# Float64 weights split in 512-column pieces, with the steps of the split dealt out anew over three engines

## Chip, cores and metric

The kernel runs on one core of one Trainium2 chip. The metric is the device time of one execution, in microseconds (us). Before the change three runs took 2179.05, 2179.7 and 2180.8 us, median 2179.7 us.

## What is computed

The reference chains an attention and two feed-forward layers over 4 x 576 = 2304 tokens of 512 numbers:

```python
attn_out = _attn_ref(q, k, v)        # 8 heads of 64; window 32, heads 4-7 with stride 4
x = attn_out.transpose(0, 2, 1, 3).reshape(B * S, H * D)     # [2304, 512]
# _moe_ref
xn = x / sqrt(mean(x * x) + 1e-6) * rms_g
g = xn @ w_gate                      # w_gate, w_val [512, 1536]
x = (g * sigmoid(g) * (xn @ w_val)) @ w_out                  # w_out [1536, 512]
# _moe2_ref
P = exp(x @ wg); 8 times: normalise P over experts and over tokens
out = sum over 8 experts of P[:, e] * (relu(x @ w1[e]) @ w2[e])
```

The three matrices of the first feed-forward layer (w_gate, w_val, w_out) reach the kernel as float64 numbers, 8 bytes each. All others are float32.

## The kernel before

TensorE multiplies in a rounded 32-bit format (float32r). To keep float32 accuracy each operand is split into a high part and a low part, and each product takes three passes: high x high, high x low, low x high (`PASSES`). A float64 weight is first made into a float32 one on the chip, then split.

**The weights.** The three matrices are cut into 36 weights of 128 x 512 numbers, numbered 0 to 35. `moe1_weights` makes them in this order: for each third fg = 0, 1, 2 of the inner dimension, four of w_gate (g0 to g3), four of w_val (v0 to v3), and four of w_out. A name such as v02 is row block 0 of w_val, third 2; o8 is row block 8 of w_out. `split_double` (from L241) makes one of them. Numbers 0 to 25 are *wide*: one DMA of 512 KB (L250) brings all 512 columns into a tile of the pool wx. Numbers 26 to 35 (g22, g32, v02 to v32, o8 to o11) are *narrow*: two DMAs of 256 KB each (L262) bring half of the columns into a staging tile, three of which are in the pool stg and two in apool. In both cases the conversion then runs in two halves of 256 columns:

- ScalarE takes the absolute value of the float64's upper word (L271) into a scratch tile m;
- VectorE clamps it (L272), shifts and masks it (L274) and puts sign and top bit back (L277);
- ScalarE scales the lower word (L281) and GpSimd adds it to m (L282), which is now the float32 weight;
- the high part is a rounded copy of m: on ScalarE (L284) for even numbers, on GpSimd (L286) for odd ones;
- the low part is m minus the high part (L289): on GpSimd for every third number, on VectorE for the others.

The scratch m of weights 0 to 11 and of the narrow ones is one of three 256-column buffers of apool. Weights 12 to 25 use a wx tile as scratch, one for two weights (`m_slot`).

**The order of the work.** Every engine runs its instructions in the order of its own queue. A scheduler sets these orders when the program is built, with a simulated timeline; only SP, which issues the loads, is scheduled by hand-written code order from L501 to L586. The program order around the change: attention of block 0 and 1 (tiles 0 to 4; `att_tile`) among the first weights; the first third of both blocks (`gemm_h` makes the products pg and pv and the hidden h, `gemm_out` the output product po); the second third; the last third of block 0; attention of block 2 (tiles 5 to 7); the last third of block 1. After that come blocks 2 to 7, with all weights resident, and then the second layer, which loads and splits float32 weights (L458 to L489).

```python
def gemm_h(blk, f):      # 4 row blocks x 3 passes each for pg, then pv
    ...
        nc.scalar.activation(hf, pg[:, :n], AF.Silu)
        nc.vector.tensor_tensor(out=hf, in0=pv[:, :n], in1=hf, op=ALU.mult)
```

pg_1_11 is the gate product of block 1 for inner block 11, po_0_2_0 the first output product of block 0 in the last third.

Of the kernel before, what the change touches and what calls it, by code (L numbers as in the profile page):

```python
# [8 lines left out]
F32 = mybir.dt.float32  # L9
F32R = mybir.dt.float32r  # L10
AF = mybir.ActivationFunctionType
ALU = mybir.AluOpType
# [5 lines left out]
P = 128  # L18
# [8 lines left out]
LEAST, MOST = (struct.unpack("f", struct.pack("I", w))[0] for w in (0x38100000, 0x47EFFFFF))  # L27
# [5 lines left out]
def attention_moe_kernel(  # L33
# [14 lines left out]
    nc = tc.nc  # L48
# [6 lines left out]
    stg = ctx.enter_context(tc.tile_pool(name="stg", bufs=3))  # L55
# [14 lines left out]
    apool = ph1.enter_context(tc.tile_pool(name="apool", bufs=1))  # L70
# [167 lines left out]

    m_slot = []

    def split_double(pool, src, name, number, hi_eng, lo_eng):  # L241

        wide = number < 26
        w = pool.tile([P, 2, 512], F32R, tag="w", name=f"w_{name}")
        if wide:
            st = wx.tile([P, 2, 512], F32R, tag="w", name=f"sd_{name}")
            raw = st.rearrange("p s n -> p (s n)").bitcast(U32)
            nc.sync.dma_start(raw.bitcast(U64), src)  # L250
            if number >= 12:
                if number % 2 == 0:
                    m_slot.append(wx.tile([P, 2, 512], F32R, tag="w", name=f"m_{name}").bitcast(F32))
                scratch = m_slot[-1][:, number % 2, :].rearrange("p (j n) -> p j n", j=2)
        for j in range(2):
            cols = slice(256 * j, 256 * j + 256)
            if wide:
                words = raw[:, 512 * j : 512 * j + 512]
            else:
                pool_st, bufs = (stg, 3) if (2 * number + j) % 5 < 3 else (apool, 2)  # L260
                words = pool_st.tile([P, 512], U32, tag="st", name=f"sd_{name}_{j}", bufs=bufs)
                nc.sync.dma_start(words.bitcast(U64), src[:, cols])  # L262
            words = words.rearrange("p (n t) -> p n t", t=2)
            low, high = words[:, :, 0], words[:, :, 1]
            if wide and number >= 12:
                mf = scratch[:, j, :]
            else:
                mf = apool.tile([P, 256], F32, tag="m", name=f"m_{name}_{j}", bufs=3)
            m = mf.bitcast(U32)

            nc.scalar.activation(mf, high.bitcast(F32), AF.Abs)  # L271
            nc.vector.tensor_scalar(out=mf, in0=mf, scalar1=LEAST, scalar2=MOST, op0=ALU.max, op1=ALU.min)  # L272

            nc.vector.tensor_scalar(  # L274
                out=m, in0=m, scalar1=3, scalar2=0x3FFFFFF8, op0=ALU.logical_shift_left, op1=ALU.bitwise_and
            )
            nc.vector.scalar_tensor_tensor(  # L277
                out=m, in0=high, scalar=0xC0000000, in1=m, op0=ALU.bitwise_and, op1=ALU.bitwise_or
            )

            nc.scalar.activation(low, low, AF.Copy, scale=2.0**-29)  # L281
            nc.gpsimd.tensor_tensor(out=m, in0=m, in1=low, op=ALU.add)  # L282
            if hi_eng is nc.scalar:
                nc.scalar.copy(w[:, 0, cols], mf)  # L284
            else:
                hi_eng.tensor_scalar(  # L286
                    out=w[:, 0, cols], in0=mf, scalar1=1.0, scalar2=1.0, op0=ALU.mult, op1=ALU.mult
                )
            lo_eng.tensor_tensor(out=w[:, 1, cols], in0=mf, in1=w[:, 0, cols].bitcast(F32), op=ALU.subtract)  # L289
        return w  # L290

    def split_weight(pool, src, name, *how):
        if src.dtype == U64:
            return split_double(pool, src, name, *how)
        st = stg.tile([P, 512], F32, tag="st", name=f"st_{name}", bufs=3)
        nc.sync.dma_start(st, src)
        w = pool.tile([P, 2, 512], F32R, tag="w", name=f"w_{name}")
        nc.scalar.copy(w[:, 0, :], st)
        nc.vector.tensor_tensor(out=w[:, 1, :], in0=st, in1=w[:, 0, :].bitcast(F32), op=ALU.subtract)
        return w  # L300
# [3 lines left out]
    def moe1_weights():  # L304
        cnt = 0

        def one(dst, key, pool, src, name):
            nonlocal cnt
            dst[key] = split_weight(
                pool, src, name, cnt,  # L310
                (nc.scalar, nc.gpsimd)[cnt % 2], (nc.gpsimd, nc.vector, nc.vector)[cnt % 3],
            )
            cnt += 1

        for fg in range(3):
            for dst, src, nm in ((gw, w_gate, "g"), (vw, w_val, "v")):
                for kt in range(4):
                    one(
                        dst, (kt, fg), wr if fg == 0 else wx,
                        src[kt * P : kt * P + P, fg * 512 : fg * 512 + 512], f"{nm}{kt}{fg}",  # L320
                    )
                    yield
            for f in range(4 * fg, 4 * fg + 4):
                one(ow, f, wr if fg < 2 else wx, w_out[f * P : f * P + P, :], f"o{f}")
                yield
# [572 lines left out]
```

## Time and profile before

| | |
|---|---|
| median of three runs | 2179.7 us (2179.05 to 2180.8) |
| the profiled execution | 2179.37 us |
| its span (first to last instruction) | 2177.6 us |
| outside the span | 1.8 us |
| mean granted clock of TensorE | 0.98 |

Engines in the profile: PE is TensorE's matrix multiplication, PEld its weight loads (beside PE), DVE VectorE, ACT ScalarE, POOL GpSimd, SP SyncE, which issues DMAs. A busy time counts only instructions that compute. PEclk is the clock that TensorE was granted, as a share of its full 2.4 GHz. L272 is line 272 of the kernel. A wait is put down to what came last.

### The profile page before, as it was taken

The numbers are of one execution on the slowest core, as the hardware profiler recorded it, in microseconds if no ns is written. First come the engines' busy times: TensorE is split into PE (matmuls) and PEld (weight loads), VectorE is DVE, ScalarE is ACT, GpSimd is POOL, SyncE is SP. The second block draws the span as 40 slices with busy tenths as digits, with TensorE's granted clock in tenths as the row PEclk, the third lists the DMA queues.
The fourth block names the chain that finished last, engine by engine and source line by source line (L and its number), as shares of the span: only waits on it lengthen the run. The fifth ranks groups of instructions, "written<-read, shape, count | busy, mean of one in ns | idle before, by whom it ended". The sixth has DMA issues, their size and how long they took to land.

```text
span 2177.6 us, 32755 instructions
## 1 busy us (share of the span) xinstructions
PE 2095.7 (96%) x12546; PEld 1904.3 (87%) x12546; DVE 1240.5 (57%) x2159; ACT 901.4 (41%) x1952; POOL 772.4 (35%) x853
## 2 busy tenths in 40 slices
PE   4899999999998699999999999999999999999999
PEld 3788999999986589998998899899989998899887
DVE  7987333423463565665656466656656565566553
ACT  4655443434354233443334444433434444344431
POOL 3774111111275242433333334333332334333320
PEclk7899999999998899999999999999999999999999
DMA  9233212210133111221122122212221122122110
GB/s 267 94 110 110 59 56 58 68 45 26 56 117 113 49 63 49 78 78 54 63 88 87 50 68 78 73 55 67 78 85 66 63 78 68 53 75 78 59 40 34
DMA packets 83246, 160.92 MB, mean 74 GB/s; under 512 B 10384, under 2 KB 18192, under 8 KB 83088
## 3 DMA queue, kind: packets, MB, share of 16 engines
q1 hardware_dynamic: 76128, 140.63, 20.3%
q10 hardware_dynamic: 6960, 18.19, 3.0%
q8 instruction: 98, 1.61, 0.3%
q14 instruction: 60, 0.49, 0.1%
HBM read 149.34 MB, written 9.44 MB: 73 GB/s over the span
## 4 chain that ended last, share of the span: by engine, by line
PE 87%; DVE 5%; DMA 3%; issue 2%; ACT 1%; POOL 1%; SPq 1%; ACTq 0%; POOLq 0%; DVEq 0%
PE py L742 36%; PE pa L685 18%; PE pb L685 9%; PE po L342 6%; PE pg L368 6%; PE pv L368 5%; PE pc L685 5%; PE psX L182 1%; DMA sd_v<-in_w_val 1%; PE psS L138 1%; DMA st_w<-in_w 1%; DMA first<-in_kt 0%; DVE m_o L272 0%; DVE m_g L277 0%; DMA sd_g<-in_w_gate 0%
## 5 line engine op out<-in xcount | busy, mean ns | idle before, releaser
L742 PE MATMUL py<-w,h 128*128 128x512 f32 x3456 | 867.4, 395 | 1.2 <-DVE acc L763 0.6
L742 PEld LDWEIGHTS py<-w,h 128*128 128x128 f32 x3456 | 648.6, 189 | 120.9 <-DVE acc L763 1.0
L489 POOL TENSOR_TENSOR w<-st_w,w 128x512 fp32r<-128x512 f32 x184 | 238.1, 1314 | 351.9 <-ACT w L488 342.2
L763 DVE SCALAR_TENSOR_TENSOR acc<-py,Pm,acc 128x512 f32<-128x512 f32 x264 | 194.1, 748 | 273.0 <-PE py L742 272.6
L685 PE MATMUL pa<-x_b,w 128*128 128x384 f32 x1152 | 257.2, 340 | 12.4 <-ACT w L471 7.1
L458 POOL TENSOR_TENSOR w1s<-w1r 128x256 f32<-128x256 f32 x92 | 75.0, 816 | 511.6 <-DVE w L472 511.6
L685 PE MATMUL pa<-x_t,w 128*128 128x384 f32 x1152 | 244.6, 337 | 0.0
L685 PEld LDWEIGHTS pa<-x_b,w 128*128 128x128 f32 x1152 | 208.5, 190 | 25.5 <-ACT w L471 8.7
L685 PEld LDWEIGHTS pa<-x_t,w 128*128 128x128 f32 x1152 | 206.7, 188 | 14.2 <-ACT pq L714 0.2
L368 PE MATMUL pv<-xn,w_v 128*128 128x320 f32 (+1 forms) x1152 | 185.9, 300 | 6.3 <-DVE hf L381 2.2
L383 POOL TENSOR_TENSOR h<-hf,h 128x256 fp32r<-128x256 f32 (+1 forms) x96 | 80.4, 839 | 314.3 <-ACT h L382 311.6
L488 ACT CAST w<-st_w 128x512 fp32r<-128x512 f32 x184 | 108.6, 621 | 198.5 <-PE pa L685 85.5
L368 PE MATMUL pg<-xn,w_g 128*128 128x320 f32 (+1 forms) x1152 | 182.6, 299 | 4.6 <-ACT xn L232 4.3
L342 PE MATMUL po<-h,w_o 128*128 128x320 f32 (+1 forms) x1152 | 178.4, 299 | 6.0 <-DVE w_o L289 3.3
L368 PEld LDWEIGHTS pv<-xn,w_v 128*128 128x128 f32 x1152 | 163.4, 190 | 11.1 <-DVE hf L381 3.1
L342 PEld LDWEIGHTS po<-h,w_o 128*128 128x128 f32 x1152 | 160.5, 189 | 12.0 <-DVE w_o L289 3.7
L368 PEld LDWEIGHTS pg<-xn,w_g 128*128 128x128 f32 x1152 | 163.2, 191 | 7.5 <-issue 6.1
L472 DVE TENSOR_TENSOR w<-w1r,w 128x512 fp32r<-128x512 f32 x92 | 111.8, 1215 | 50.0 <-ACT w L471 49.8
L472 DVE TENSOR_TENSOR w<-w1s,w 128x512 fp32r<-128x512 f32 x184 | 123.4, 696 | 27.6 <-ACT w L471 25.9
L471 ACT CAST w<-w1s 128x512 fp32r<-128x512 f32 x184 | 111.3, 620 | 61.6 <-PE pc L685 18.2
L697 ACT ACTIVATE h<-pq 128x384 fp32r<-128x384 f32 x96 | 50.4, 525 | 184.2 <-DVE pq L726 183.5
L685 PE MATMUL pb<-x_t,w 128*128 128x384 f32 x576 | 126.5, 338 | 0.0
(157 smaller groups left out, 2734.1 us busy)
## 6 DMA issues: line engine op xcount, KB each, us to landing
st_w<-in_w SPq DMA_DIRECT2D x184, 256.0 KB, 2.7
w1r<-in_w SPq DMA_DIRECT2D x184, 256.0 KB, 2.8
vbd<-in_vt ACTq DMA_DIRECT2D x30, 256.0 KB, 3.8
kbd<-in_kt ACTq DMA_DIRECT2D x30, 208.0 KB, 3.8
sd_g<-in_w_gate SPq DMA_DIRECT2D x10, 512.0 KB, 7.0
xr<-x2d SPq DMA_DIRECT2D x12, 384.0 KB, 3.5
sx<-x2d SPq DMA_DIRECT2D x24, 192.0 KB, 2.4
out<-acc SPq DMA_DIRECT2D x18, 256.0 KB, 2.1
```

Source lines behind the costliest of these rows:

```text
L342: nc.tensor.matmul(po[:, :n], lhsT=ow[f][:, a, dc * P : dc * P + P], rhs=hs[blk, f][:, bb, :n], start=k == 0, stop=k == 11,)
L368: nc.tensor.matmul(ps[:, :n], lhsT=w[kt, fg][:, a, fo * P : fo * P + P], rhs=xn[:, kt, bb, :n], start=k == 0, stop=k == 11,)
L383: nc.gpsimd.tensor_tensor(out=h[:, 1, :n], in0=hf, in1=h[:, 0, :n].bitcast(F32), op=ALU.subtract)
L458: nc.gpsimd.tensor_tensor(out=s1, in0=a21, in1=a22f, op=ALU.add)
L471: nc.scalar.copy(hi, src)
L472: nc.vector.tensor_tensor(out=lo, in0=src, in1=hi.bitcast(F32), op=ALU.subtract)
L488: nc.scalar.copy(w[:, 0, :], st)
L489: nc.gpsimd.tensor_tensor(out=w[:, 1, :], in0=st, in1=w[:, 0, :].bitcast(F32), op=ALU.subtract)
L685: nc.tensor.matmul(ps[:, :TH], lhsT=w1s[ch, a, kt][:, s, q * P : q * P + P], rhs=xc[b, kt][:, t, :TH], start=first and k == 0, stop=k == 5 ...
L697: nc.scalar.activation(h[:, 0, :], src, AF.Relu)
L742: nc.tensor.matmul(ps, lhsT=hh[u, f, th][:, a, jj * P : jj * P + P], rhs=w2s[ch, f][:, bb, :], start=k == 0, stop=k == 11,)
L763: nc.vector.scalar_tensor_tensor(out=acc[j], in0=ps, scalar=Pm[:, tt, e : e + 1], in1=acc[j], op0=ALU.mult, op1=ALU.add)
```

## The change

Wide weights are converted in one piece of 512 columns, narrow ones still in two of 256. The clamp moves from VectorE to GpSimd (min first, then max). All high parts go to ScalarE, all low parts to VectorE. The scratch in apool becomes two buffers of 512 columns in place of three of 256. The staging of narrow weights loses a buffer: three in stg and one in apool.

```diff
-    def split_double(pool, src, name, number, hi_eng, lo_eng):
+    def split_double(pool, src, name, number):
...
-                scratch = m_slot[-1][:, number % 2, :].rearrange("p (j n) -> p j n", j=2)
-        for j in range(2):
-            cols = slice(256 * j, 256 * j + 256)
+                scratch = m_slot[-1][:, number % 2, :]
+        n = 512 if wide else 256
+        for j in range(512 // n):
+            cols = slice(n * j, n * j + n)
             if wide:
-                words = raw[:, 512 * j : 512 * j + 512]
+                words = raw
             else:
-                pool_st, bufs = (stg, 3) if (2 * number + j) % 5 < 3 else (apool, 2)
+                pool_st, bufs = (stg, 3) if (2 * number + j) % 4 < 3 else (apool, 1)
...
-                mf = scratch[:, j, :]
+                mf = scratch
             else:
-                mf = apool.tile([P, 256], F32, tag="m", name=f"m_{name}_{j}", bufs=3)
+                mf = apool.tile([P, 512], F32, tag="m", name=f"m_{name}_{j}", bufs=2)[:, :n]
...
-            nc.vector.tensor_scalar(out=mf, in0=mf, scalar1=LEAST, scalar2=MOST, op0=ALU.max, op1=ALU.min)
+            nc.gpsimd.tensor_scalar(out=mf, in0=mf, scalar1=MOST, scalar2=LEAST, op0=ALU.min, op1=ALU.max)
...
-            if hi_eng is nc.scalar:
-                nc.scalar.copy(w[:, 0, cols], mf)
-            else:
-                hi_eng.tensor_scalar(
-                    out=w[:, 0, cols], in0=mf, scalar1=1.0, scalar2=1.0, op0=ALU.mult, op1=ALU.mult
-                )
-            lo_eng.tensor_tensor(out=w[:, 1, cols], in0=mf, in1=w[:, 0, cols].bitcast(F32), op=ALU.subtract)
+            nc.scalar.copy(w[:, 0, cols], mf)
+            nc.vector.tensor_tensor(out=w[:, 1, cols], in0=mf, in1=w[:, 0, cols].bitcast(F32), op=ALU.subtract)
```

In the changed kernel the clamp is L273, the shift L275, the sign step L278, the add L283, the high part L284, the low part L285 and the narrow load L263; lines after the split stand seven higher than before.

The change also moves instructions. On VectorE, around the weights v21 and v31 of the middle third, before (m_v21 is the scratch tile that both weights share; xs_5 belongs to attention tile 5; hf is `gemm_h`'s product):

```order
L277 SCALAR_TENSOR_TENSOR m_v21_1242<-sd_v21_1240,m_v21_1242 128x256
L272 TENSOR_SCALAR m_v21_1242<-m_v21_1242 128x256
L274 TENSOR_SCALAR m_v21_1242<-m_v21_1242 128x256
L277 SCALAR_TENSOR_TENSOR m_v21_1242<-sd_v31_1260,m_v21_1242 128x256
L194 TENSOR_TENSOR xs_5_2236<-psX_5_2219,rs_5_2206 128x512
L289 TENSOR_TENSOR w_v31_1259<-m_v21_1242,w_v31_1259 128x256 x2
L381 TENSOR_TENSOR hf_0_4_1384<-pv_0_4_1358,hf_0_4_1384 128x256
```

and in the changed kernel:

```order
L275 TENSOR_SCALAR m_v21_1086<-m_v21_1086 128x512
L278 SCALAR_TENSOR_TENSOR m_v21_1086<-sd_v21_1084,m_v21_1086 128x512
L155 TENSOR_TENSOR sc_7_2338<-psS_7_2321,cst_89 128x512
L158 TENSOR_REDUCE mx_7_2340<-sc_7_2338 128x8
L159 TENSOR_TENSOR sc_7_2338<-sc_7_2338,mx_7_2340 128x512
L285 TENSOR_TENSOR w_v21_1083<-m_v21_1086,w_v21_1083 128x512
L162 TENSOR_REDUCE sm_7_2344<-sc_7_2338 128x8
L163 TENSOR_SCALAR sm_7_2344<-sm_7_2344 128x8
L165 RECIPROCAL rs_7_2347<-sm_7_2344 128x8
L275 TENSOR_SCALAR m_v21_1086<-m_v21_1086 128x512
L278 SCALAR_TENSOR_TENSOR m_v21_1086<-sd_v31_1096,m_v21_1086 128x512
L285 TENSOR_TENSOR w_v31_1095<-m_v21_1086,w_v31_1095 128x512
```

One instruction stands for two, the clamp L272 is gone from this engine, and the steps of attention tile 7 have moved up among the two weights.

On SP, the loads behind g31, the last gate weight of the middle third, before:

```order
L250 DMA sd_g31_1182<-in_w_gate 128x512
L250 DMA sd_v01_1201<-in_w_val 128x512
L262 DMA sd_v02_1_1823<-in_w_val 128x256
L262 DMA sd_v12_0_1835<-in_w_val 128x256
L250 DMA sd_v11_1221<-in_w_val 128x512
L262 DMA sd_v12_1_1846<-in_w_val 128x256
L250 DMA sd_v21_1240<-in_w_val 128x512
```

and in the changed kernel:

```order
L250 DMA sd_g31_1050<-in_w_gate 128x512
L263 DMA sd_v02_0_1592<-in_w_val 128x256
L263 DMA sd_v02_1_1603<-in_w_val 128x256
L250 DMA sd_v01_1061<-in_w_val 128x512
L250 DMA sd_v11_1073<-in_w_val 128x512
L250 DMA sd_v21_1084<-in_w_val 128x512
```

Both halves of the narrow weight v02 now stand between g31 and v01, and those of v12 have moved behind the wide loads.

On TensorE, where block 0's last output product first reads w_o11, the last of the 36 weights, before:

```order
L368 MATMUL pg_1_10_2472<-xn_1_490,w_g32_1788 128x320 x3
L368 MATMUL pv_1_10_2473<-xn_1_490,w_v02_1811 128x320 x3
L368 MATMUL pv_1_10_2473<-xn_1_490,w_v12_1834 128x320
L342 MATMUL po_0_2_0_2380<-h_0_11_2173,w_o11_1972 128x256 x2
L342 MATMUL po_0_2_1_2395<-h_0_11_2173,w_o11_1972 128x256 x2
```

and in the changed kernel:

```order
L361 MATMUL pg_1_11_2284<-xn_1_418,w_g32_1568 128x320 x3
L361 MATMUL pv_1_11_2285<-xn_1_418,w_v02_1591 128x320 x3
L361 MATMUL pv_1_11_2285<-xn_1_418,w_v12_1614 128x320 x3
L361 MATMUL pv_1_11_2285<-xn_1_418,w_v22_1637 128x320 x3
L361 MATMUL pv_1_11_2285<-xn_1_418,w_v32_1660 128x320 x3
L138 MATMUL psS_8_2405<-kbd_90,q_8_2356 32x128
L335 MATMUL po_0_2_0_2160<-h_0_11_1953,w_o11_1752 128x256 x2
L335 MATMUL po_0_2_1_2175<-h_0_11_1953,w_o11_1752 128x256 x2
```

The first read of w_o11 has moved back, behind all the products of block 1 (pg_1_11 and pv_1_11) and the first one of attention tile 8.

## Rows read from the trace of the kernel before

**Rows 1.** The page: busy time, share of the span and instructions of each engine.
```profile
PE 2095.7 (96%) x12546; PEld 1904.3 (87%) x12546; DVE 1240.5 (57%) x2159; ACT 901.4 (41%) x1952; POOL 772.4 (35%) x853
```

**Rows 2.** Stretches: us, PE, PEld, DVE, ACT, POOL busy (instructions), PEclk, DMA share, GB/s.
```profile
55.00:80.00 25.00, 18.14 (x197) 14.60 (x196) 24.86 (x65) 18.30 (x57) 18.07 (x25) 0.73 0.39 126
80.00:105.00 25.00, 23.01 (x161) 21.31 (x159) 25.00 (x60) 12.98 (x34) 18.81 (x25) 1.00 0.13 39
105.00:125.00 20.00, 19.71 (x151) 18.10 (x151) 13.72 (x33) 13.07 (x34) 12.53 (x18) 0.91 0.74 263
125.00:153.00 28.00, 24.34 (x181) 23.20 (x181) 26.08 (x59) 15.33 (x47) 19.90 (x28) 1.00 0.08 20
153.00:184.00 31.00, 27.02 (x223) 23.40 (x221) 29.62 (x66) 19.41 (x46) 22.56 (x31) 1.00 0.48 141
184.00:600.00 416.00, 415.60 (x3734) 405.84 (x3735) 157.71 (x363) 164.71 (x368) 84.72 (x107) 1.00 0.18 54
```

**Rows 3.** TensorE's waits, 55 to 205 us: total us, times, longest us.
```profile
PE po L342 <- DVE w_o L289: 3.3, 2, 1.9
```

**Rows 4.** Stretches for L272, L274, L277, L289 (DVE, POOL); last row L277 alone.
```profile
0.00:205.00 205.00, 32.69 (x72) 0.88 0.49 148
0.00:205.00 205.00, 30.45 (x72) 0.88 0.49 148
0.00:205.00 205.00, 36.16 (x72) 0.88 0.49 148
0.00:205.00 205.00, 28.19 (x48) 20.02 (x24) 0.88 0.49 148
55.00:105.00 50.00, 11.60 (x23) 0.86 0.26 83
```

**Rows 5.** Gate weights, by operation: ns min/median/max, first and last start, forms.
```profile
L271 ACT ACTIVATE m_g<-sd_g x24: 413/430/457, 14.1 to 152.5; 128x256 f32<-128x256 f32 x24
L272 DVE TENSOR_SCALAR m_g<-m_g x24: 235/284/957, 14.6 to 153.8; 128x256 f32<-128x256 f32 x24
L274 DVE TENSOR_SCALAR m_g<-m_g x24: 276/282/834, 14.9 to 154.6; 128x256 uint32<-128x256 uint32 x24
L277 DVE SCALAR_TENSOR_TENSOR m_g<-sd_g,m_g x24: 407/417/1000, 15.5 to 155.1; 128x256 uint32<-128x256 uint32 x24
L282 POOL TENSOR_TENSOR m_g<-m_g,sd_g x24: 723/756/994, 16.1 to 155.7; 128x256 uint32<-128x256 uint32 x24
L286 POOL TENSOR_SCALAR w_g<-m_g x12: 399/452/927, 21.5 to 156.8; 128x256 fp32r<-128x256 f32 x12
L289 DVE TENSOR_TENSOR w_g<-m_g,w_g x12: 405/512/971, 22.3 to 155.7; 128x256 fp32r<-128x256 f32 x12
```

**Rows 6.** Timeline from 139.4 us: start, us, engine, line, operation.
```profile
139.51 0.77 POOL L282 TENSOR_TENSOR m_o<-m_o,sd_o 128x256 uint32<-128x256 uint32 x1
139.61 0.83 DVE L274 TENSOR_SCALAR m_o<-m_o 128x256 uint32<-128x256 uint32 x1
```

**Rows 7.** Costliest groups, forms apart: busy us, mean ns of one, idle time before.
```profile
L489 POOL TENSOR_TENSOR w<-st_w,w 128x512 fp32r<-128x512 f32 x184 | 238.1, 1314 | 351.9 <-ACT w L488 342.2 <-issue 6.8 <-PE pc L685 2.9
L472 DVE TENSOR_TENSOR w<-w1s,w 128x512 fp32r<-128x512 f32 x184 | 123.4, 696 | 27.6 <-ACT w L471 25.9
L488 ACT CAST w<-st_w 128x512 fp32r<-128x512 f32 x184 | 108.6, 621 | 198.5 <-PE pa L685 85.5 <-DMA st_w<-in_w 75.2 <-PE py L742 32.9
L760 POOL TENSOR_SCALAR acc<-acc,Pm 128x512 f32<-128x512 f32 x6 | 4.4, 744 | 6.7 <-DVE Pm L672 4.2 <-DVE acc L757 2.5
```

**Rows 8.** Timeline: the first abs of v02 (ScalarE), the last low parts of o11 (VectorE).
```profile
153.88 0.44 ACT L271 ACTIVATE m_v<-sd_v 128x256 f32<-128x256 f32 x1 [0.97 <-DVE w_g L289]
195.49 0.94 DVE L289 TENSOR_TENSOR w_o<-m_o,w_o 128x256 fp32r<-128x256 f32 x2 [0.47 <-POOL w_o L286]
```

**Rows 9.** Timeline of SP: two neighbouring issues, of v01 and of v02 and v12.
```profile
64.03 0.33 SPq L250 DMA_DIRECT2D sd_v<-in_w_val  x1
102.74 2.07 SPq L262 DMA_DIRECT2D sd_v<-in_w_val  x2
```

More of the change, by code (lines that the diff above doesn't have):

```diff
@@ L308, in one @@
             nonlocal cnt
[L309 to L312, printed above, removed]
+            dst[key] = split_weight(pool, src, name, cnt)
             cnt += 1
```

## The prediction

> **What bounds the kernel now.** I read the page's busy times first, then the same by stretch, then the wait lists and single instructions of the stretch that was not full. Over the whole span TensorE is busy 96% [rows 1], and from 184 to 600 us it is idle only 0.4 us of 416 [rows 2]; faster weight conversion can't help there. What is open lies before 184 us. Up to 55 us I take the start to be set by the arriving inputs and leave it alone. From 55 to 184 us [rows 2] the reader should see three things. TensorE is idle 6.9 + 2.0 + 0.3 + 3.7 + 4.0 = 16.9 us. Its granted clock is 0.73 in the first stretch and 0.91 in the third, between the two levels of 1.2 and 2.4 GHz, after pauses; counted as work not done that is 0.27 x 18.1 + 0.09 x 19.7 = 6.7 us. And VectorE is full or nearly so in four of the five: 24.9 of 25, 25.0 of 25, 26.1 of 28, 29.6 of 31. So conversion sets the pace there, and **some 23.6 us is the most that this change can bring**, if TensorE's total work stays. TensorE's waits name it: the longest one, up to 205 us, is for a weight's low part [rows 3].
>
> Why is VectorE full? The three mask instructions and its low parts take 32.69 + 30.45 + 36.16 + 28.19 = 127.5 us [rows 4]. At their undisturbed durations, 0.28, 0.28, 0.41 and 0.41 us (the medians and shortest ones in [rows 5]), 72, 72, 72 and 48 of them take 20.2 + 20.2 + 29.5 + 19.7 = 89.6 us. The other 38 us are waits inside the instruction: the longest L272 takes 0.96 us. [rows 6] shows one: L274 starts 0.10 us after a GpSimd add of 0.77 us and ends only 0.16 us after it. The Trainium skill, "SBUF — State Buffer", section "Who interferes with whom", says that such a VectorE instruction and a GpSimd instruction that reads SBUF take the shared port pair for their whole length, and the later one stands still. The rows agree.
>
> **The change, part by part**, for one weight of 512 columns, undisturbed. *VectorE, wide weights (numbers 0 to 25).* Before: 2 x (0.28 + 0.28 + 0.41) + two thirds of 2 x 0.41 = 2.49 us. After: one L274, one L277, one low part. Two-input instructions of 512 columns take 0.70 us (L472, [rows 7]). A 512-column mask shift has no row: below it is 0.28 (256 columns), above it 0.70; the steps of the two-input one (0.41 to 0.70) halved give 0.42, which I take, since it is at 256 columns already the quicker one. Sum 1.8 us, 0.7 less. Instructions that can meet a lock fall from 7.3 to 3 per weight, but each GpSimd instruction is longer. Now a weight loses 38/36 = 1.05 us; at 0.14 us per instruction it would lose 0.4, at twice that 0.8. I take 0.75, so 1.0 us less per wide weight, bounds 0.7 to 1.35.
>
> *GpSimd, wide.* Before: 2 x 0.75 for the add, 2 x 0.45 / 2 for the high part (half of the weights), 2 x 0.75 / 3 for the low part (a third; its GpSimd form taken as long as the add): 1.5 + 0.45 + 0.5 = 2.45 us [rows 5]. After: one add of 1.31 (L489, [rows 7]) and the clamp. The clamp reads one tensor of 512 columns: L760, a TENSOR_SCALAR too, takes 0.74 in the mean [rows 7]; half of two-input work at 0.66 and the full 1.31 bound it. I take 0.74, the row of its own kind: 1.31 + 0.74 = 2.05 us, 0.4 less. The Trainium skill, "GPSIMD Engine Reference", section "Engine selection", speaks against the step: elementwise min and max belong on VectorE, though a one-input operation on GpSimd is about line rate. By it alone the clamp costs GpSimd more than it saves VectorE. Here GpSimd is busy 18.1 and 18.8 of 25 us where VectorE has no slack [rows 2], and sheds more than it gets.
>
> *ScalarE.* Every high part is now its own, but of 512 columns at once. Before, a half had an abs of 0.43 (L271, [rows 5]), a scaling and in half of the weights a copy, which I take to be as long: 2 x (0.43 + 0.43 + 0.43 / 2) = 2.15 us per weight. After, three of 0.62 (L488, a 512-column cast, [rows 7]): 1.9. It is busy 18.3 of 25 us at most [rows 2]: no cost.
>
> *Narrow weights (26 to 35).* VectorE per weight 2.49 to 2 x (0.28 + 0.41 + 0.41) = 2.2 us, GpSimd 2.45 to 2 x (0.45 + 0.75) = 2.4. But the scratch buffers go from three to two, and the staging ones from five to four. A half now passes ScalarE 0.43, GpSimd 0.45, VectorE 0.28 + 0.41, GpSimd 0.75, ScalarE 0.43, VectorE 0.41 = 3.2 us, its partner queues behind both GpSimd steps (1.2 us), and on ScalarE the next abs stands behind a scaling that waits for a load. So a pair needs at least 3.2 + 1.2 = 4.4 us, and with the waits of three busy engines I take 5.5, an estimate with 4.4 below and 8 above. Today the eight last weights take from 153.9 us (first abs) to 196.4 us (last low part) [rows 8], 5.3 us each. **So the narrow stretch gets no faster.**
>
> *Queues.* On SP the second half of v02 waits now as before for g22's staging slots, and v11 to o7 stand behind it: nothing is issued between 64.4 and 102.7 us [rows 9]. In the change v01 stands behind both halves of v02; before, it was issued at 64.0 us. This wait ends when g22 is converted, so it moves with VectorE, and so do v01 to o7. On VectorE attention tiles 6 and 7 stand among the instructions of v11 to v31 in the change; that is work for TensorE while it waits for v31, and work ahead of v31 on VectorE.
>
> **The sum.** From 55 to 105 us VectorE does 23 halves (L277, [rows 4]), 11.5 weights (TensorE idle 8.8, clock loss 4.9 us). Ten of them save 1.0 us each; I take 8, since attention work of tiles 2 to 5 with its own chain stands between them. From 105 to 125 us TensorE is full: 0. From 125 to 184 us TensorE is idle 7.6 us; o4 to o7, g02 and g12 save 6 us, but nine narrow weights at 5.5 instead of 5.3 us give 2 back, and one more I leave off for the queues: 3. After 205 us nothing changes, since TensorE is full and each engine's order ends in the same long tail. **Total 11 us.** The profiled execution took 2179.4 us, of which 2177.6 are the span; the median of the three runs is 2179.7, so 0.3 apart. 2179.4 - 11 = **2168.4 us**.
>
> **The rivals.** *Nearly all of the idle time goes.* If the locks fall with the number of instructions (1.35 us per wide weight) and the narrow loop keeps near 4.5 us, VectorE and GpSimd are off the path and TensorE sets the pace from 60 us: 18 to 23 us gained, about 2159. For it: both lose work. Against it: the SP wait and the attention tiles' loads stay.
>
> *Nothing measurable.* The clamp costs 1.31 us per 512 columns, GpSimd takes 2.6 us per wide weight, more than now, and holds the ports longer; the locks cost 1.0 us again instead of 0.75. The wide weights then save 0.4 us, of which 4 us show up, and the narrow loop, at 5.6 instead of 5.3 us, takes 3 back: 2178. Against it is the row of L760. The Trainium skill's rule on engine selection points this way; the measured 0.74 us of the one-input operation on this engine does not.
>
> *Slower: the two-buffer loop decides.* If a narrow weight takes 8 us, because the two halves in flight wait in three in-order engines and for a load, nine of them from about 143 us end at 215. Before, w_o11 could be read no earlier than 196.4, where its last low part ends [rows 8]. In the change some 64 more matmuls stand ahead of it on TensorE, 32 of the block's own (the rest of pv_1_10, all of pg_1_11 and pv_1_11) and about as many of an attention tile; at the 0.11 us that one takes in the mean from 184 to 600 us (415.6 us, 3734 of them [rows 2]) that is 7 us, so at 204 it would still come in time. This rival loses 11 us: 2190. It decides from (204 - 143)/9 = 6.8 us per weight on. For it: fewer buffers, longer chain. Against it: the chain is only 3.2 us without queues.
>
> *The change does not do what it says* is ruled out by the order: the 72 clamps leave VectorE (26 x 2 + 10 x 2), and 26 + 10 x 2 = 46 stand on GpSimd.
>
> **How the numbers follow.** Forecast (5 to 17 us gained) 0.50; most of the idle time 0.17; nothing measurable 0.20; slower 0.13. About 0.2%, 4.4 us, is what a measurement of this kernel can tell from no change. Faster by more than that: 0.50 + 0.17 + 0.04 from the edge of the third case = 0.71; within it 0.17; slower 0.12. The range reaches from 2157 (22 us gained, near the most there is) to 2180, taking in the third case and leaving out the slower one. The likeliest case alone spans 2162 to 2174.
>
> **What would show it.** Right: in the changed profile the clamp takes near 0.7 us, the add 1.31, VectorE is no longer full from 55 to 105 us, SP issues v01 about 8 us earlier than 102.7, and from 55 us to the end of the conversion TensorE's idle time and clock loss are some 13 us in place of 23.6. The narrow weights still take 5 to 6 us each. Wrong: a clamp above 1 us, mean VectorE durations that grow by more than the halved count saves, TensorE waiting long on the low parts of v12 to v32 or of o8 to o11, or a change of time beyond 205 us.

## Result and profile after

The changed kernel takes **2198.69 us** (median of five runs, 2195.92 to 2200.36) against 2180.8 us (2179.05 to 2182.02) of the kernel before: a ratio of 1.0081, 95% interval 1.0066 to 1.0096. It is slower by 18 us. I had forecast 2168.4 us (2157 to 2180) and given slower 12%: the forecast was wrong in its sign. The profiled execution took 2198.02 us, its span is 2195.9 us, 18.3 us longer than before, the mean granted clock of TensorE 0.974.

The page of the changed kernel, busy times (answers to [rows 1]):

```profile
PE 2106.3 (96%) x12546; PEld 1916.6 (87%) x12546; DVE 1218.0 (55%) x2033; ACT 908.2 (41%) x1912; POOL 762.1 (35%) x813
```

VectorE is busy 22 us less, GpSimd 10 us less, ScalarE 7 us more. On the first two the work did get smaller. The stretches (answers to [rows 2], same columns, with the last one cut at 230 us) tell where the time goes all the same:

```profile
55.00:80.00 25.00, 20.68 (x199) 18.91 (x199) 20.75 (x37) 19.59 (x44) 15.67 (x17) 0.80 0.28 96
80.00:105.00 25.00, 23.29 (x203) 22.19 (x204) 19.32 (x38) 16.64 (x36) 13.79 (x14) 1.00 0.27 89
105.00:125.00 20.00, 17.78 (x171) 15.80 (x166) 9.12 (x17) 11.44 (x23) 7.95 (x9) 0.91 0.45 145
125.00:153.00 28.00, 20.43 (x165) 16.59 (x154) 16.50 (x29) 16.42 (x33) 10.47 (x13) 0.63 0.50 157
153.00:184.00 31.00, 28.44 (x199) 27.39 (x197) 21.75 (x37) 12.96 (x29) 19.07 (x20) 1.00 0.06 16
184.00:230.00 46.00, 37.36 (x262) 35.43 (x263) 32.45 (x70) 24.74 (x67) 22.00 (x36) 0.85 0.33 106
```

Add TensorE's idle time and its clock loss in each stretch, as the prediction did. From 55 to 105 us it loses 10.1 us instead of 13.8, so there the change gains 3.6 us, and VectorE is no longer full. From 105 to 125 us it loses 3.8 instead of 2.1; from 125 to 153 us 7.6 idle and 0.37 x 20.4 = 7.6 of clock, 15.1 instead of 3.7; from 153 to 184 us 2.6 instead of 4.0; from 184 to 230 us 8.6 + 0.15 x 37.4 = 14.2, where before it was full from 184 us on. In all 46 us instead of 24, that is 22 more, against a span that is 18.3 us longer; the clock has two digits, so more agreement can't be asked. Note what the engines do from 105 to 153 us: VectorE is busy 25.6 of 48 us, ScalarE 27.9, GpSimd 18.4. **No engine is the bound, and TensorE waits.** The granted clock of 0.63 from 125 to 153 us, between the levels of 1.2 and 2.4 GHz, follows these pauses. At 230 us the loss is complete: from there to 2100 us TensorE is busy 1839.9 us of 1870, before 1839.2.

TensorE's waits from 55 to 205 us (answers to [rows 3]):

```profile
PE pv L361 <- ACT w_v L284: 15.6, 8, 3.2
PE pv L361 <- ACT hf L373: 3.2, 3, 2.3
PE psXT L222 <- DVE xs L216: 1.9, 1, 1.9
```

The longest wait, 3.3 us in total before, is now 15.6 us, and it is for the high part of a w_val weight, on ScalarE, the engine for which the prediction had said "no cost". ScalarE's timeline over two of these weights, v01 and v11 (start, us, engine, line, operation, idle before it and what ended that; ACTq is ScalarE's queue issuing a DMA):

```profile
111.19 0.65 ACT L272 ACTIVATE m_v<-sd_v 128x512 f32<-128x512 f32 x1
111.74 0.67 ACT L282 ACTIVATE sd_v<-sd_v 128x512 uint32<-128x512 uint32 x1
112.90 0.43 ACT L344 COPY partial<-po 128x320 f32<-128x320 f32 x1 [0.48 <-PE po L335]
114.66 0.43 ACT L344 COPY partial<-po 128x320 f32<-128x320 f32 x1 [1.33 <-PE po L335]
116.42 0.33 ACTq L112 DMA_DIRECT2D q<-in_qt  x1
116.78 0.47 ACTq L117 DMA_DIRECT2D kbd<-in_kt  x1
117.30 0.62 ACT L284 CAST w_v<-m_v 128x512 fp32r<-128x512 f32 x1 [2.21 <-PE psS L138]
...
119.77 0.67 ACT L272 ACTIVATE m_v<-sd_v 128x512 f32<-128x512 f32 x1
...
125.54 0.47 ACTq L126 DMA_DIRECT2D vbd<-in_vt  x1
126.06 0.62 ACT L284 CAST w_v<-m_v 128x512 fp32r<-128x512 f32 x1 [2.87 <-PE psX L182]
```

And GpSimd's timeline for the same two, the adds on whose end L284 depends:

```profile
114.25 1.29 POOL L283 TENSOR_TENSOR m_v<-m_v,sd_v 128x512 uint32<-128x512 uint32 x1 [1.61 <-ACT partial L344]
...
122.56 1.31 POOL L283 TENSOR_TENSOR m_v<-m_v,sd_v 128x512 uint32<-128x512 uint32 x1 [1.42 <-issue]
```

The weight v01 is added up at 115.5 us and v11 at 123.9 us. Their high parts start at 117.3 and 126.1 us, because ahead of them in ScalarE's queue stand loads of the next attention tile's q, k and v, which are not issued before TensorE has read the tile there now. Then the low part follows on VectorE, and v11's abs stands behind all of it. v01 takes from 111.2 to 119.2 us (end of its low part), v11 from 119.8 to 127.4.

### The profile page after: what moved, and what is told of

The parts are those of the page before. It is cut to its first block, busy times and chain, and to the rows that moved or that the text cites. A ratio compares the mean times of both kernels' runs of the same rounds, so it can differ in the third digit from the quotient of the medians.

```text
span 2195.9 us, 32531 instructions
## 1 busy us (share of the span) xinstructions
PE 2106.3 (96%) x12546; PEld 1916.6 (87%) x12546; DVE 1218.0 (55%) x2033; ACT 908.2 (41%) x1912; POOL 762.1 (35%) x813
## 4 chain that ended last, share of the span: by engine, by line
PE 88%; DVE 2%; DMA 1%; ACT 1%; issue 1%; POOL 1%; ACTq 0%; SPq 0%; POOLq 0%; DVEq 0%
PE py L735 36%; PE pa L678 18%; PE pb L678 9%; PE pv L361 6%; PE po L335 6%; PE pg L361 6%; PE pc L678 5%; PE psS L138 1%; PE psX L182 1%; DVE h L691 0%; DMA w1r<-in_w 0%; DMA sx<-x2d 0%; PE psXT L222 0%; PE psT L169 0%; DMA st_w<-in_w 0%
## 5 line engine op out<-in xcount | busy, mean ns | idle before, releaser
L678 PE MATMUL pa<-x_b,w 128*128 128x384 f32 x1152 | 256.2, 339 | 12.8 <-ACT w L464 11.5
L678 PEld LDWEIGHTS pa<-x_b,w 128*128 128x128 f32 x1152 | 208.7, 190 | 24.8 <-ACT w L464 12.8
L361 PE MATMUL pv<-xn,w_v 128*128 128x320 f32 (+1 forms) x1152 | 191.5, 308 | 20.8 <-ACT w_v L284 15.6
L361 PE MATMUL pg<-xn,w_g 128*128 128x320 f32 (+1 forms) x1152 | 187.3, 304 | 6.8 <-ACT xn L232 5.1
L361 PEld LDWEIGHTS pv<-xn,w_v 128*128 128x128 f32 x1152 | 169.0, 197 | 26.4 <-ACT w_v L284 18.6
L361 PEld LDWEIGHTS pg<-xn,w_g 128*128 128x128 f32 x1152 | 167.6, 196 | 10.3 <-ACT xn L232 5.5
L465 DVE TENSOR_TENSOR w<-w1r,w 128x512 fp32r<-128x512 f32 x92 | 111.2, 1208 | 42.6 <-ACT w L464 42.2
```

What stands on the lines that cost most here:

```text
L361: nc.tensor.matmul(ps[:, :n], lhsT=w[kt, fg][:, a, fo * P : fo * P + P], rhs=xn[:, kt, bb, :n], start=k == 0, stop=k == 11,)
L465: nc.vector.tensor_tensor(out=lo, in0=src, in1=hi.bitcast(F32), op=ALU.subtract)
L678: nc.tensor.matmul(ps[:, :TH], lhsT=w1s[ch, a, kt][:, s, q * P : q * P + P], rhs=xc[b, kt][:, t, :TH], start=first and k == 0, stop=k == 5 ...
```

## Experiments

"The other order" is below the order in which the scheduler puts the steps when the clamp is on VectorE (the second experiment). Each was timed in three rounds beside the kernel before, whose medians there were 2179.45 to 2181.75 us; every ratio is against it. A weight is "ready" when its low part ends.

**1. Attention tiles 6 and 7 queued behind v31.** In the change tile 6 stands among v01 and v11, and tile 7 among v21 and v31.

```diff
-        nc.vector.tensor_tensor(out=sc, ...)                 # L155
+        with tc.issue_after(low_part["v31"]) if n in (6, 7) else nullcontext():
+            nc.vector.tensor_tensor(out=sc, ...)
```

> The changed kernel with one edge in the order added: the first VectorE step of attention tiles 6 and 7 is queued behind the low part of weight v31, so that the two tiles no longer stand among v01 to v31. Nothing else is edited. Theory A (the change lost its time because the new order put tiles 6 and 7 among the weights of the middle third, and each weight's steps now stand in line behind waiting steps of a tile): v31 is done near 127 us instead of 144.1, and the time is 2170 to 2183 us. Theory B (dearer conversion: the clamp on GpSimd, all high parts on ScalarE, one more hand-over per weight): no more than 4 us gained, 2194 to 2199. Theory C (two scratch buffers and four staging slots bound the narrow weights, my rival of the prediction): o11 still ends 75 to 80 us after v31 but shifted with it, the narrow weights 5 us each, and the time stays near 2195 because their end still comes too late.

Measured: 2192.99 us, 1.0062 (1.0044 to 1.008). v31 is ready at 133.4 us instead of 144.1, but w_o11 at 223.7 as before (223.9). Of the 18 us only 5.7 are back: what the tiles did not cost ahead of v31 they mostly cost behind it. The place of the tiles alone is not the cause.

**2. The clamp back on VectorE**, the rest of the change kept.

```diff
-            nc.gpsimd.tensor_scalar(out=mf, in0=mf, scalar1=MOST, scalar2=LEAST, op0=ALU.min, op1=ALU.max)
+            nc.vector.tensor_scalar(out=mf, in0=mf, scalar1=MOST, scalar2=LEAST, op0=ALU.min, op1=ALU.max)
```

> The changed kernel with the clamp alone put back on VectorE (512 columns for wide weights). In its order tiles 6 and 7 come after v31 without any added edge. Theory A: v31 near 127 us and a time of 2170 to 2183, within 4 us of the run with the held tiles. Theory B with the clamp as the cause: clearly faster than the run with the held tiles, by over 5 us. Theory C: 2194 to 2199.

Measured: 2181.98 us, 1.0011 (1.0001 to 1.002). One line brings 16.7 of the 18 us back. But this line also makes the scheduler put TensorE's, VectorE's and ScalarE's instructions in another order, so it does not yet say whether the clamp's engine or the order does it.

**3. The kernel before with block 2's attention moved ahead** (tile 6 then stands between v01 and v11).

```diff
-    run(block_att(2))
+    with tc.high_priority(offset=1500):
+        run(block_att(2))
```

> The kernel before, with attention block 2 given a higher scheduling priority, so that tile 6 stands between v01 and v11 and tile 7 behind v31 on VectorE. The conversion, its columns, engines and buffers are those of before. Theory A: v31 ends 8 to 18 us later than the 125.5 us of before, and the time is 2186 to 2199 us. Theories B and C: 2178 to 2184, as before.

Measured: 2175.64 us, 0.9983 (0.9973 to 0.9992): faster than both kernels. Tile 6 among these weights does no harm by itself. Of tile 7 this run says less: it begins at 133.0 us, behind v31 (ready at 129.5), but its step L194 comes only at 183.5 us. Other instructions change places here too.

**4. The tiles' loads issued from GpSimd's queue** in place of ScalarE's, in the changed kernel.

```diff
-                (lambda: set0.load_qk(tn + 1, nc.scalar)) if more else None,
-                (lambda: set0.load_v(tn + 1, nc.scalar)) if more else None,
+                (lambda: set0.load_qk(tn + 1, nc.gpsimd)) if more else None,
+                (lambda: set0.load_v(tn + 1, nc.gpsimd)) if more else None,
```

> The changed kernel with the loads of attention tiles 6 and later issued from GpSimd instead of ScalarE, the order of VectorE as in the change. In the changed kernel the high parts of g31, v01, v11, v21 and v31 stood 1.0 + 1.8 + 2.2 + 2.1 + 1.0 = 8 us behind such loads on ScalarE. Theory A, if those loads are the way by which the tiles hold the weights: 6 to 8 us gained, 2190 to 2193. Theory A, if the tile's other steps hold them as much: under 3 us gained, 2195 to 2199. Theories B and C: 2195 to 2199, or slower by what the issue costs GpSimd.

Measured: 2199.7 us, 1.0094 (1.0079 to 1.0109). Nothing is won: v31 ends at 145.9 us. The loads that I had just read as the cause on ScalarE were only the last thing to hold the weight up. The weights now wait elsewhere, ahead of the shift on VectorE: between v01's clamp and its shift lie 2.9 us, in the change 0.3.

**5 and 6. Order and clamp apart.** A table gives, for TensorE, VectorE and ScalarE up to w_o11, the order of all instructions but the clamps, and each is tied behind its forerunner on its own engine (an order of issue, with no wait for a result). Experiment 5 has the clamp on GpSimd as the change has, in the other order; experiment 6 the clamp on VectorE, in the change's order.

```diff
+    for e, ranks in ORDER.items():
+        own = [i for i in traced if i.engine == kinds[e] and i.name not in clamps and ...]
+        chain = [own[k] for k in ranks]
+        for a, b in zip(chain, chain[1:]):
+            tc.add_manual_dep(b, a.name, mybir.DependencyInfo(mybir.DependencyClass.NoSync, ...), reason="order")
```

> The changed kernel, clamp on GpSimd, with the order of the run that has the clamp on VectorE imposed on TensorE, VectorE (but for the clamps) and ScalarE up to the last weight; GpSimd's own order and the clamps' places are left to the scheduler. Theory D (the order in which the steps stand costs the time: the changed scheduler run queues a weight's shift and high part behind other steps): within 5 us of that run's 2182.0, and the mean wait between a wide weight's clamp and its shift falls from 2.4 us to under 1 us. Theory E (the clamp on GpSimd costs it itself: its place in GpSimd's queue, its length and the locks): 2193 to 2200, with the wait of 2.4 us still there or moved ahead of the clamp. In between would share it out.

> The mirror: clamp on VectorE, with the order of the changed kernel imposed on TensorE, VectorE (but for the clamps) and ScalarE up to the last weight. Theory D: 2193 to 2200, near the 2198.7 of the change. Theory E: 2180 to 2186.

Measured: 2180.64 us, 1.0000 (0.9991 to 1.0009), and 2197.68 us, 1.0081 (1.0066 to 1.0096). With experiment 2 and the change itself this is a full square:

| us | change's order | other order |
|---|---|---|
| clamp on GpSimd | 2198.7 | 2180.6 |
| clamp on VectorE | 2197.7 | 2182.0 |

Down a column the clamp's engine is worth 1.4 us at most; along a row the order is worth 16 to 18 us. GpSimd's own steps and SP's loads are not in the table; by the traces they too stand in nearly the same order down a column and differ along a row, so "order" means that of all the queues together. **This is the loss: not what the instructions cost, but in which order the in-order engines take them.** The stretch from 105 to 153 us shows it too; experiment 6 (columns as in [rows 2]):

```profile
105.00:153.00 48.00, 36.46 (x303) 31.15 (x303) 25.66 (x51) 26.94 (x53) 12.11 (x13) 0.72 0.49 150
```

and experiment 5:

```profile
105.00:153.00 48.00, 41.01 (x308) 36.87 (x307) 27.95 (x46) 26.61 (x53) 24.86 (x26) 0.89 0.23 70
```

ScalarE and VectorE are as busy in one as in the other, while TensorE's pauses and clock differ. TensorE's wait list from 55 to 230 us begins, for experiment 6,

```profile
PE pv L369 <- ACT w_v L292: 14.2, 8, 3.1
```

and for experiment 5

```profile
PE pv L369 <- ACT w_v L292: 4.6, 4, 1.9
```

ScalarE's timeline of experiment 5 over v01 and v11 (abs L280, high part L292) is to be held against that of the change above:

```profile
101.82 0.66 ACT L280 ACTIVATE m_v<-sd_v 128x512 f32<-128x512 f32 x1
...
106.12 0.62 ACT L292 CAST w_v<-m_v 128x512 fp32r<-128x512 f32 x1 [0.30 <-POOL m_v L291]
106.65 0.68 ACT L280 ACTIVATE m_v<-sd_v 128x512 f32<-128x512 f32 x1
...
110.68 0.62 ACT L292 CAST w_v<-m_v 128x512 fp32r<-128x512 f32 x1 [0.59 <-POOL m_v L291]
```

The high part now waits for its own weight's add and for nothing else, and v11's abs follows directly on v01's high part: 9 us from v01's abs to v11's high part, 14.9 us in the change. Not all four weights go so smoothly: v01 to v31 are ready at 107.5, 112.0, 119.7 and 126.8 us, and v21's high part stands behind loads of tile 6 here too.

**7 and 8. The narrow loads of v02 to v32 and o8 to o11 put behind g12's load on SP**, in the changed kernel (7) and in the kernel before (8).

```diff
-            nc.sync.dma_start(raw.bitcast(U64), src)
+            load[name] = nc.sync.dma_start(raw.bitcast(U64), src).ins
...
-                nc.sync.dma_start(words.bitcast(U64), src[:, cols])
+                with tc.issue_after(load["g12"]) if name[0] != "g" else nullcontext():
+                    nc.sync.dma_start(words.bitcast(U64), src[:, cols])
```

> The changed kernel with the loads of the narrow weights of the last third queued on SP behind the load of g12; the orders of VectorE, ScalarE and TensorE stay, but for steps that wait for these loads. In the change v02's two loads, which wait for a staging slot until 98.9 us, keep v01 to v31 from being issued before 100.7 us. Theory F (this wait on SP holds the middle third): v01 is issued some 30 us earlier, v31 ends at least 8 us before 144.1, 5 to 15 us gained. Theory D: v01 to v31 are converted in the same places of the same queues, under 3 us gained.

> The same edit on SP's order in the kernel before, where v02's second half and v12 wait from 64.4 to 102.7 us ahead of v11 to o7. Theory F: v11 is issued well before 100 us and v31 ends some 5 us before 125.5; TensorE's idle time from 80 to 125 us is only 2.3 us, so 0 to 6 us gained, 2174 to 2180. Theory D: 2178 to 2182.

Measured: 2199.61 us, 1.0087 (1.0072 to 1.0102), and 2179.02 us, 0.9997 (0.9988 to 1.0007). In the changed kernel SP issues v02's loads and then four wide ones (start, us, the first row of two issues, the second of four):

```profile
98.89 1.77 SPq L263 DMA_DIRECT2D sd_v<-in_w_val  x2
100.72 19.83 SPq L250 DMA_DIRECT2D sd_v<-in_w_val  x4
```

and in experiment 7

```profile
61.77 58.48 SPq L251 DMA_DIRECT2D sd_v<-in_w_val  x4
```

The loads of v01 and v11 move from 100.7 and 101.2 to 61.8 and 87.6 us (v21's and v31's stay), and the time does not follow: v31 is ready at 144.9 us. In the kernel before, v11's load moves from 104.9 to 65.0 us, v31 is ready at 126.8 us in place of 125.5, and the time is the same; there the other engines' orders change as well, so that run is the weaker of the two. The wait on SP decides neither time.

**9, 10, 13, 14. Which part of the order.** The same table, cut: the change's order up to the low part of g31 and the other order from there (9), the reverse (10), and the same with the cut at v31 (13 and 14).

```diff
-    "DVE": [0, 1, 2, ...],      # one order to the end
+    "DVE": [0, 1, 2, ...],      # ranks of one order up to the cut, then what is left in the ranks of the other
```

> The changed kernel; TensorE, VectorE and ScalarE keep the change's own order up to the low part of g31 and then take the other order (that of the run with the clamp on VectorE). In the change g31 ended at 110.0 us, with the other order at 101.0, and v31 at 144.1 against 126.8: about half of the 17 us arise before g31 and half behind it. If a late start stays late: v31 near 136 us and 2188 to 2192 us. If only the place of attention tiles 6 and 7 behind g31 matters: 2180 to 2184. If only the order before g31 matters: 2195 to 2199.

> The mirror: the other order up to the low part of g31, then the change's own, with attention tiles 6 and 7 among v01 to v31. If both parts cost: g31 near 101, v31 near 135 us, 2188 to 2192 us. If only the place of tiles 6 and 7 matters: 2195 to 2199. If only the order before g31 matters: 2180 to 2184.

> The changed kernel; TensorE, VectorE and ScalarE keep the change's own order up to the low part of v31, then take the other order. If the loss arises in the middle third, between g31 and v31 (34 us in the change, 26 with the other order) and is only carried on behind it: 2194 to 2199 us, o11 still some 80 us behind v31. If the order of o4 to o11 makes it: 2183 to 2188.

> The mirror: the other order up to the low part of v31, then the change's own, in which the steps of attention tiles 6 and 7 that the other order has not yet done come first, between v31 and o4. If the middle third makes the loss: v31 near 127 us and 2181 to 2187, the upper end for the tiles that stand ahead of o4. If the later order does: 2192 to 2198.

Measured: 9: 2185.37 us, 1.0024 (1.0015 to 1.0033); 10: 2196.05, 1.007 (1.0053 to 1.0087); 13: 2193.48, 1.0062 (1.0047 to 1.0077); 14: 2205.46, 1.0119 (1.0102 to 1.0136). Against experiment 5 the change's order up to g31 alone costs 4.7 us, though g31 is ready at 108.4 instead of 101.0 us. From g31 on alone it costs 15.4 us, though g31 is then ready at 100.2. Up to v31 it costs 12.8 us. So most of the loss sits in the steps behind g31. Experiments 5, 9, 13 and the change differ from one to the next in one stretch only, and the loss falls on all three: some 5 us up to g31, 8 between g31 and v31, 5 behind v31, each good to about 3 us. From v31 to w_o11 the change takes no longer (79.8 us) than experiments 5 (79.6) and 13 (79.2): the 17.5 us by which w_o11 is later in the change than in 5 are nearly all there at v31, 144.1 against 126.8 us. Experiment 14 is no clean mirror: its cut leaves tiles 6 and 7 as one block between v31 (ready at 125.1 us) and o4 (160.1), and it is the slowest of all.

**11. All weights in halves of 256 columns**, with the scratch and staging buffers of before; clamp, high and low parts as in the change.

```diff
-        n = 512 if wide else 256
+        n = 256
...
-                mf = apool.tile([P, 512], F32, tag="m", name=f"m_{name}_{j}", bufs=2)[:, :n]
+                mf = apool.tile([P, 256], F32, tag="m", name=f"m_{name}_{j}", bufs=3)
```

> The changed kernel with all weights converted in two halves of 256 columns again and the buffers of before (three scratch buffers, five staging slots); clamp on GpSimd, high parts on ScalarE, low parts on VectorE as in the change. In its order attention tile 6 stands before v01 and tile 7 between v21 and v31 on VectorE. Theory G (tiles among the weights of the middle third are costly where a weight is one piece, since nothing of a second piece is in flight while a step waits for a tile; in the kernel before, in halves, early tiles cost v31 only 4 us and no time): v31 near 130 us, 2178 to 2188. If the place of the tiles costs whatever the piece: v31 near 142 and 2194 to 2200.

Measured: 2186.39 us, 1.0037 (1.0023 to 1.0052). The engines' new shares alone, without the larger pieces, also end slower than before, though less so: v31 is ready at 140.7 us, as late as the theory of the tiles' place had it, while the time lies in the range of theory G. Its order is again another one, so this does not isolate the size.

**12. Clamp on VectorE as in 2, block 2's attention ahead as in 3.**

> The kernel with the clamp back on VectorE (512-column pieces, 2182.0 us) with attention block 2 given the same higher priority as the run of the kernel before with early tiles (2175.6 us there): tile 6 comes between v01 and v11, tile 7 between v21 and v31. Theory G, or the place of the tiles alone: v31 near 140 us instead of 124.1, 2192 to 2199. If early tiles help as they did in the kernel before: 2176 to 2182.

Measured: 2177.92 us, 0.9993 (0.9984 to 1.0002). Tile 6 stands between v01 and v11 as in the change, v31 is ready at 130.5 us, and the kernel is no slower than before. Attention among the weights can be harmless in 512-column pieces too, so theory G falls; tile 7, as in experiment 3, begins early (128.5 us) but reaches L194 only at 169.5 us. Experiment 3 stays the fastest version.

**What the runs have in common.** When w_o11's low part ends, the time is nearly told: 196.4 us before, 200.9 in 8 (2179.0 us), 202 to 210 in experiments 2, 3, 5, 9 and 12 (2175.6 to 2185.4 us), 212.5 in 11 (2186.4), 223 to 226 in the change and in 1, 4, 6, 7, 10 and 13 (2193.0 to 2199.7), 230 in 14. And the slow ones, except 1, have one thing in common: attention tile 7 is all but over by 137 to 147 us. In the change, VectorE's first step of tile 7 (L155), its last but a few (L194) and the first step of tile 8:

```profile
134.12 0.69 DVE L155 TENSOR_TENSOR sc<-psS,cst 128x512 f32<-128x512 f32 x1 [2.59 <-PE psS L138]
141.66 0.69 DVE L194 TENSOR_TENSOR xs<-psX,rs 128x512 f32<-128x512 f32 x1 [1.37 <-PE psX L182]
227.00 0.69 DVE L155 TENSOR_TENSOR sc<-psS,cst 128x512 f32<-128x512 f32 x1
```

In experiment 5 tile 7 lasts from 179.9 to 204.6 us (L162 and L201 there):

```profile
179.90 0.69 DVE L162 TENSOR_TENSOR sc<-psS,cst 128x512 f32<-128x512 f32 x1 [0.78 <-PE psS L145]
204.62 0.69 DVE L201 TENSOR_TENSOR xs<-psX,rs 128x512 f32<-128x512 f32 x1 [0.52 <-PE psX L189]
```

In the change TensorE's last step of tile 7 comes at 150 us and its first of tile 8 at 224.6 us, so it has no attention between to fill the waits for the narrow weights. From 184 to 205 us its longest wait is for the high parts of the narrow w_val weights:

```profile
PE pv L361 <- ACT w_v L284: 8.8, 3, 3.2
```

This is a regularity over the runs; no run moved tile 7 and nothing else. Which single step is the costly one in the change's order **stays open**.

## Why the prediction was wrong

**The prices were right.** The costliest groups of the changed kernel, forms apart, and the clamp of the middle weights:

```profile
L283 POOL TENSOR_TENSOR m_g<-m_g,sd_g 128x512 uint32<-128x512 uint32 x10 | 14.5, 1450 | 2.3 <-ACT first L174 1.2 <-DVE m_g L278 1.1
L273 POOL TENSOR_SCALAR m_g<-m_g 128x512 f32<-128x512 f32 x10 | 7.2, 721 | 15.4 <-ACT m_g L272 15.4
L273 POOL TENSOR_SCALAR m_v<-m_v 128x512 f32<-128x512 f32 x8 | 5.0, 621 | 24.2 <-ACT m_v L272 24.2
L284 ACT CAST w_v<-m_v 128x512 fp32r<-128x512 f32 x8 | 4.9, 612 | 15.7 <-PE psS L138 8.4 <-PE psX L182 4.1 <-issue 3.2
L275 DVE TENSOR_SCALAR m_v<-m_v 128x512 uint32<-128x512 uint32 x8 | 4.6, 573 | 0.5 <-POOL m_v L273 0.5
L278 DVE SCALAR_TENSOR_TENSOR m_v<-sd_v,m_v 128x512 uint32<-128x512 uint32 x8 | 5.5, 686 | 0.1
```

The clamp takes 0.62 to 0.72 us (0.74 taken), the add 1.45 with its stretched ones, 1.29 to 1.31 undisturbed (1.31), the sign step 0.69 (0.70), the high part 0.61 (0.62). Of the shift the same line's undisturbed ones take 0.42 us, as taken; the mean of 0.57 holds waits inside the instruction. In the mean of the 26 wide weights VectorE's three instructions take 2.34 us, where 1.8 + 0.75 = 2.55 was taken. VectorE's relief from 55 to 105 us came: 40.1 busy of 50 us, 49.9 before.

**The narrow loop was right too.** The first abs of v02 and the last low part of o11 in the changed kernel, and TensorE behind 205 us (columns as in [rows 2]):

```profile
181.49 0.45 ACT L272 ACTIVATE m_v<-sd_v 128x256 f32<-128x256 f32 x1 [0.86 <-DVE w_g L285]
223.52 0.43 DVE L285 TENSOR_TENSOR w_o<-m_o,w_o 128x256 fp32r<-128x256 f32 x1 [1.08 <-ACT w_o L284]
205.00:230.00 25.00, 25.00 (x200) 24.27 (x200) 17.77 (x42) 13.96 (x38) 10.33 (x17) 0.96 0.33 108
```

From 181.5 to 223.9 us the eight last weights take 42.4 us, 5.3 each: before 5.3 [rows 8], forecast 5.5, and 6.8 the point from which the slower rival decides. It forecast 2190 us from a w_o11 that TensorE has to wait for. The loop was not slower, it began 27.6 us later than before. And TensorE does not wait for w_o11: it is full from 205 us on, and the first product that reads w_o11 starts at 225.0 us, behind the first step of tile 8. What TensorE waited for longest, from 184 to 205 us, were the high parts of the narrow w_val weights. That the time moved the way of this rival was luck: its mechanism did not occur.

**The step that failed is "Queues"**, and with it the sum. It said of tiles 6 and 7 among v11 to v31: "that is work for TensorE while it waits for v31, and work ahead of v31 on VectorE", and the sum took 1 us for all the queues. Experiments 5 and 6 put 16 to 18 us on the order of which this is a part; some 8 of them arise between g31 and v31, where the two tiles stand. In these orders v01 to v31 run as a chain, one weight after the other through ScalarE, GpSimd, VectorE, GpSimd, ScalarE, VectorE. Experiment 1, where no step of tile 6 or 7 stands among them, has v11 to v31 ready at 124.3, 128.9 and 133.4 us, some 4.5 us from weight to weight. In the change v01 to v31 are ready at 119.2, 127.4, 136.9 and 144.1 us, 7 to 10 us apart: between two steps of one weight an engine must first do attention steps that wait for TensorE themselves, as the timelines above show. What one engine saves did not shorten this chain.

**"Ten of them save 1.0 us each; I take 8" failed by itself as well.** Experiment 5 has the change's work and prices in a good order, and it gains nothing: 2180.64 against 2179.56 us. From 55 to 105 us TensorE loses 9.8 us there instead of 13.8, so 4 of the 8 us come; in the next stretch, with 5.3 instead of 2.1 us, it loses most of them again:

```profile
105.00:125.00 20.00, 15.96 (x150) 14.23 (x148) 7.19 (x14) 9.27 (x21) 7.93 (x9) 0.92 0.27 74
```

It idles 4.0 us of 20, before 0.3 [rows 2], and VectorE is busy only 7.2. I had written "TensorE is full: 0" for this stretch, as if it would stay full when the work ahead of it got done sooner. The premise was that the full VectorE sets the pace of the conversion. In experiment 5 it is busy 39.9 of the 50 us in place of 49.9, and the conversion gets no lasting lead from it: g31 is ready at 101.0 us (100.5 before), v11 at 112.0 (115.7), v31 at 126.8 (125.5). The one wait that I had shown for the premise was 3.3 us, of 16.9 us idle. The 6 us for o4 to o7, g02 and g12 did not come either: from v31 to the first abs of v02 pass 34.6 us there and 37.4 in the change, 28.4 before. What was late next behind a faster VectorE was the weights' way from engine to engine, and I did not ask. Which part of the change (the larger pieces, the new shares or the fewer buffers) keeps it from being faster was not isolated and stays open.

**SP.** Said: the wait moves with VectorE, v01 is issued about 8 us before 102.7. Measured 100.7, 2 us before; and by experiment 7 it doesn't matter.

**The rivals.** "Nothing measurable" gave 2178 us through a dear clamp. The clamp is not dear, and its engine is worth 1.4 us at most. The Trainium skill, "GPSIMD Engine Reference", section "Engine selection", puts an elementwise max on a tile on VectorE, not on GpSimd. The times of one clamp agree (medians of the 26 wide weights: 0.62 us on GpSimd in the change, 0.43 on VectorE in experiment 2); the time of the kernel does not care.

**What would have shown it.** The text named as signs of an error a clamp above 1 us, grown VectorE durations, "TensorE waiting long on the low parts of v12 to v32 or of o8 to o11", or a change beyond 205 us. TensorE waits long, but for the high parts of the narrow w_val weights, and only up to 205 us; beyond that the change loses about 1 us, of clock. The other two did not occur. The order of instructions stood there before the run, and ScalarE's queue was not among the excerpts: its prediction was "no cost" from its busy share, and a busy share says nothing of what a queue stands behind.

## What to carry to other kernels

Where an automatic scheduler orders in-order queues, even a one-line move of one operation to another engine reorders the others, and that can outweigh the move (here 16 to 18 us against 1.4): before a move is judged by its time, run it in the old order, or the old work in the new order. When a stretch has no full engine and TensorE still waits, count the steps from engine to engine of one item and what stands between them in each queue, not the busy times. Where a bound is relieved, price the chain behind it before booking the gain.

## What the runs showed of the hardware

- The shift, a one-input VectorE instruction of 512 columns, takes 0.42 us undisturbed and up to 1.52 us beside a running GpSimd add; the low part 0.69 and up to 1.74 us. Halving the number of instructions did not remove these waits.
- Removing the releaser that the trace names can move the wait elsewhere and leave the time alone: ScalarE's loads (experiment 4: 2199.7 us), SP's order (experiment 7: 2199.6 us).
- The granted clock cost as much as the pauses themselves: from 125 to 153 us 7.6 us of clock beside 7.6 us of idle time.
